# Moving the pad, two weight low parts and the turns of rows in a retention and mixture-of-experts kernel

## The chip, the cores and the metric

The kernel runs on one core of a Trainium2 chip. The metric is the device time of one execution in microseconds; the median of three runs is compared. A core has TensorE (PE; matmuls and transposes), VectorE (DVE), ScalarE (ACT), GpSimd (POOL) and SyncE (SP, which here only issues transfers). Each takes its instructions in program order, and they wait for each other on semaphores.

## The reference

Retention (linear attention with a decay for each head) over 4 batches, 8 heads, 768 positions and a head size of 64, then a layer that sends each of the 3072 tokens to one of 8 experts:

```
state = gamma * state + k_t (outer) v_t ;  y_t = scale * q_t @ state        # for each batch, head, position
x = y as 3072 rows of 512
logits = normalized(x) @ normalized(expert_emb).T / tau
e = argmax(logits) ;  gate = softmax(logits)[e]
out = gate * (relu(x @ w1[e]) @ w2[e])                                      # w1: 512 x 1024, w2: 1024 x 512
```

## The kernel before

**Retention.** The 12 blocks of 256 tokens (three for each batch) run through one loop, `for m in range(NM)`. A turn of the loop makes the masked scores of block m (`scores`, `masks`), the product with the earlier state (`inter`) and within the block (`intra`), and transposes block m+1 for the next turn (`transpose_k`, `transpose_q`). `take` copies the result to SBUF as yT (ScalarE). One turn later `rows` transposes yT into token rows on VectorE (L478) and writes them to a DRAM buffer xd by four transfers (L485), and `logits_products` and `logits_rows` make the routing scores. The tile that the row transposes write has two buffers.

**Routing.** Blocks form four groups of three. For a complete group `sums`, `choose`, `add_counts` (together `pick`), `count`, `ranks` and `split_ranks` find each token's expert and its place in the expert's list; `put_scores` writes the scores to xd; `marks_of`, `mark` and `table` turn places into a table of token numbers, with matmuls of marks. Group 2 (blocks 6 to 8) is complete in block 9 (`urgent`), and its table in block 10. The last group is done after the loop.

**The first expert starts early.** From the tokens of the first nine blocks, `early_gather` fetches 288 rows of expert 0 in block 10 (three indirect gathers issued by GpSimd, L657). `pad` (L649, L651) adds to the count of expert 0 where it has fewer than 288 such tokens: it is a matmul, one instruction for ex, and three one-column instructions of VectorE on cum. In block 11 the fetched rows are transposed and split (`rows_T`).

**Split products.** Matmuls of the expert layers work on numbers split into a high and a low part: ScalarE casts (xh at L678, whi at L229, hh at L253), and a subtraction makes the low part (xl at L679, wlo at L234, hl at L256), on VectorE unless an engine is named. Each product is three matmuls: high by high, and two with a low part. `split_cast` casts one piece of 128 x 1024 weights and returns the function for its low part; `load_piece` loads a piece into one of four raw buffers. Pieces 0 to 3 are w1 of expert 0; pieces 4 to 7 are its w2. Before the change, block 10 casts pieces 0 and 1 at its beginning and 2 and 3 at its end; in block 11 the low parts of 0, 1 and 2 go to GpSimd and that of 3 to VectorE.

**After the loop** the first layer of expert 0 (`products`, advanced by `run(n)`, n matmuls at a time) is interleaved with the last group's routing, then its second layer (`layer2`), and the experts 1 to 7, in order of their size, follow. Their rows are gathered, written to DRAM (xs) and read back in quarters (xg), transposed and split.

The order on every engine (TensorE, VectorE, ScalarE, GpSimd, SP) is that of the program text; no planner changes it. SP's queue holds all loads of weights and all writes of rows in that order.

Of the kernel before, what the change touches and what calls it, by code (L numbers as in the profile page):

```python
# [24 lines left out]
P = 128  # L25
# [7 lines left out]
NE = 8  # L33
# [78 lines left out]
def retention_moe(ctx: ExitStack, tc: tile.TileContext, q, k, v, emb, tau, w1, w2, const, const16, out):  # L112
# [56 lines left out]
    def pt_():  # L169
        npt[0] += 1  # L170
        return bank(turn_of[npt[0] % len(turn_of)])
# [340 lines left out]
    def sums(g):  # L512
        nm = len(GROUPS[g])
        ps = pt_()
        for i in range(NQ):
            nc.tensor.matmul(ps[i * Q:(i + 1) * Q, :2 * nm * NE], C("quarters"),
                             parts[g][:, :nm, :, i, :NE].rearrange("p m u e -> p (m u) e"), start=True, stop=True,
                             skip_group_check=True)
        return ps[:, :2 * nm * NE].rearrange("p (n e) -> p n e", e=NE)

    def choose(g, z):
        r = span(g)
        nb = r.stop - r.start
        bc = lambda t: t.unsqueeze(2).broadcast_to([P, nb, NE])
        m = ap_.tile([P, nb], F32, name="m", bufs=1)
        nc.vector.tensor_reduce(out=m, in_=z, axis=AX.X, op=ALU.max)
        yield
        nc.vector.tensor_tensor(out=zd[:, r], in0=z, in1=bc(m), op=ALU.subtract)
        yield
        w = ap_.tile([P, nb, NE], F32, name="w", bufs=1)  # L530
        nc.vector.scalar_tensor_tensor(out=w, in0=zd[:, r], scalar=0.0,
                                       in1=C("e16").unsqueeze(1).broadcast_to([P, nb, NE]), op0=ALU.is_lt, op1=ALU.add)
        yield
        nc.vector.tensor_reduce(out=wmn[:, r], in_=w, axis=AX.X, op=ALU.min)
        yield
        nc.vector.tensor_tensor(out=oh[:, r], in0=w, in1=bc(wmn[:, r]), op=ALU.is_equal)
        yield
# [10 lines left out]
                             skip_group_check=True)  # L548
        return pr

    def add_counts(g):
        r = span(g)
        sm = ap_.tile([P, NE], F32, name="sm", bufs=1)
        nc.vector.tensor_reduce(out=sm, in_=oh[:, r].rearrange("p c e -> p e c"), axis=AX.X, op=ALU.add)
        yield
        nc.vector.tensor_tensor(out=cum[:, r.stop], in0=cum[:, r.start], in1=sm, op=ALU.add)
        yield
# [85 lines left out]

    def pad():

        ex = cp.tile([P, 1], F32, name="ex")
        pc = pt_()
        nc.tensor.matmul(pc[:, :NE], ones, cum[:, NBE], start=True, stop=True)
        nc.vector.tensor_scalar(out=ex, in0=pc[:, :1], scalar1=-1.0, scalar2=float(EARLY), op0=ALU.mult, op1=ALU.add)  # L649
        for i in range(3):  # L650
            nc.vector.scalar_tensor_tensor(  # L651
                out=cum[:, NBE, :1], in0=ex, scalar=C("tok")[:, i:i + 1], in1=cum[:, NBE, :1],
                op0=ALU.is_gt, op1=ALU.add)
# [192 lines left out]

    def pick(g, z):
        run_all(choose(g, z))
        run_all(add_counts(g))

    for m in range(NM):
        nxt = m + 1 < NM
        done = last_of.get(m - 1)
        urgent = m == NM - 3
        py_of(m)
        if m == NM - 2:
            first = [split_cast(), split_cast()]

        if m == 0:
            psc = [scores(0, u, range(2)) for u in range(2)]  # L860
            for u in range(2):
                scores(0, u, range(2, KT), psc[u])
        for u in range(2):
            o = masks(psc[u] if m == 0 else scores(m, u), u)
            if u == 0:
                i = o[0]
        if m == 0:
            for j in (*load_q(2), load_k(2)):
                after(j, i)
            nc.sync.dma_start(out=cst2, in_=const[:, _C1:])  # L870
            nc.sync.dma_start(out=cst16, in_=const16)
        if m:
            scale_ahead(m, i)
        if urgent:
            load_piece()
            load_piece()
        if m and m + 3 < NM:
            for j in load_q(m + 3):
                after(j, i)
        if m == 0:  # L880
            state(0)
            state_copy(0)
            state_sums(0)
            next(emb_steps)
            scale_ahead(0, i)
            intra(0, 0)
            intra(0, 1)
            transpose_k(1, 0)
            i = transpose_k(1, 1)
            after(load_v(2), i)  # L890
            inter(0)
            transpose_q(1, 0)
            i = transpose_q(1, 1)
            for j in (*load_q(3), load_k(3), load_v(3)):
                after(j, i)
            state(1)
            state_copy(1)
            state_sums(1)
        else:
            inter(m)  # L900
            if nxt:
                i = state(m + 1)
                state_copy(m + 1)
                if m + 3 < NM:
                    after(load_k(m + 3), i)
            if waiting is not None and m < NM - 2:
                run_all(ranks(waiting, count(waiting)))
            if urgent or not nxt:
                x = rows_turn(m - 1 - (not nxt))
                rows(m - 1 - (not nxt), x=x)  # L910
            logits_rows(m - 1, logits_products(m - 1))
            if nxt:
                if m == NM - 2:
                    marks_of(tail - 1)
                    mark(tail - 1, range(6))
                if not urgent:
                    state_sums(m + 1)
                transpose_k(m + 1, 0)
                transpose_q(m + 1, 0)
                if urgent:  # L920
                    pick(done, sums(done))
                    state_sums(m + 1)
                    put_scores(done)
                i = transpose_q(m + 1, 1)
                if m + 3 < NM:
                    after(load_v(m + 3), i)
                if m == NM - 2:
                    table(tail - 1)
                    gathered = early_gather()
                transpose_k(m + 1, 1)  # L930
                if m == NM - 2:
                    spread_v(m + 1, 0)
                if m < NM - 3:
                    rows(m - 1)
                if m in (5, 8):
                    mark(group_of[m - 3], range(6))
                if done is not None and not urgent:
                    pick(done, sums(done))
                    put_scores(done)
                intra(m, 0)  # L940
                if urgent:
                    run_all(ranks(done, count(done)))
                    split_ranks(done)
                intra(m, 1)
                if m in (5, 8):
                    table(group_of[m - 3])
                if m in (4, 7):
                    split_ranks(waiting)
                    marks_of(waiting)
                if m == NM - 2:  # L950
                    load_piece(gathered)
                    load_piece(gathered)
            else:
                pad()
                intra(m, 0)
                for f in (*first, lows[0]):
                    f(nc.gpsimd)
                lows[1]()
                intra(m, 1)
                ps = [turn_rows(xge, EROWS, kt, bank(f"pst{kt}")) for kt in range(2)]  # L960
        waiting = done
        take(m)
        if m < NM - 2:
            spread_v(m + 1, 0)
            spread_v(m + 1, 1)
        if m == NM - 2:
            spread_v(m + 1, 1)
            lows = [split_cast(), split_cast()]
        if m == 0:
            next(emb_steps)  # L970
        if m == NM - 1:
            xh0, xl0 = (hp.tile([P, KT, CAP], F32R, name=n) for n in ("xh", "xl"))
            for kt in range(KT):
                rows_T(xge, EROWS, kt, slice(0, EARLY), ps[kt] if kt < 2 else None)
            nc.gpsimd.tensor_copy(out=zs[0][:, :3], in_=xge[:, :, DM:DM + NE])

        for _ in range(LOADS.count(m)):
            load_piece()
# [20 lines left out]
    m, g = NM - 1, len(GROUPS) - 1  # L999
    pl = logits_products(m)  # L1000
    logits_rows(m, pl)
    rows(m - 1)
    load_piece()
    load_piece()
    run(11)
    first_low = split_cast()
    z = sums(g)
    run_all(choose(g, z))
    run_all(add_counts(g))
    rows(m)  # L1010
    put_scores(g)
    run(21)
    pr = count(g)
# [3 lines left out]
    for o in held:  # L1017
        o()
    first_low()
    for _ in range(9):  # L1020
        next(sort_steps)
        run(1)
# [10 lines left out]
    load_expert(2)  # L1033
    run(12)
    split()
    for j, n in EROWS:
        square(xge, n, j, j)
    run(12)
    split()
    load_piece()  # L1040
# [431 lines left out]
```

## Time and profile before

| | |
|---|---|
| median of 3 runs | 404.69 us (404.46 to 405.96) |
| profiled execution | 404.54 us; span from first to last instruction 402.7 us |
| TensorE busy | 387.2 us, 96% |
| VectorE busy | 251.5 us, 62% |
| ScalarE busy | 227.2 us, 56% |
| GpSimd busy | 134.2 us, 33% |
| transfers | 88.00 MB, mean 219 GB/s |

The busy time of an engine is a sum over stages with different limits. A row of the timeline is one instruction or several merged (x and their number): start and length in us, engine, line, operation, output from inputs, with the idle time ahead of it in brackets and what ended it. Merged rows may overlap their neighbours a little, since the instructions of an engine are pipelined.

### The profile page before, as it was taken

The numbers are of one execution on the slowest core, as the hardware profiler recorded it, in microseconds if no ns is written. First come the engines' busy times: TensorE is split into PE (matmuls) and PEld (weight loads), VectorE is DVE, ScalarE is ACT, GpSimd is POOL, SyncE is SP. The second block draws the span as 40 slices with busy tenths as digits, with TensorE's granted clock in tenths as the row PEclk, the third lists the DMA queues.
The fourth block names the chain that finished last, engine by engine and source line by source line (L and its number), as shares of the span: only waits on it lengthen the run. The fifth ranks groups of instructions, "written<-read, shape, count | busy, mean of one in ns | idle before, by whom it ended". The sixth has DMA issues, their size and how long they took to land.

```text
span 402.7 us, 9504 instructions
## 1 busy us (share of the span) xinstructions
PE 387.2 (96%) x3652; PEld 354.8 (88%) x3652; DVE 251.5 (62%) x557; ACT 227.2 (56%) x402; POOL 134.2 (33%) x145
## 2 busy tenths in 40 slices
PE   7999999999959999999999999999999999999992
PEld 3988888888739988999999999999889889999971
DVE  4565776777798958744861864487277546576400
ACT  4687787877935256463553843664485545463410
POOL 2666544551550253311702620350273062001131
PEclk9999999999969999999999999999999999999999
DMA  7999999999358669697879677887979887933121
GB/s 214 282 298 290 256 266 248 257 248 237 75 158 215 210 192 294 199 258 207 273 220 228 223 245 209 237 311 209 256 254 334 215 245 234 244 115 100 30 101 52
DMA packets 86469, 88.00 MB, mean 219 GB/s; under 512 B 9184, under 2 KB 65120, under 8 KB 86416
## 3 DMA queue, kind: packets, MB, share of 16 engines
q1 hardware_dynamic: 81936, 74.32, 66.6%
q0 software_dynamic: 4304, 12.93, 9.4%
q8 instruction: 30, 0.49, 0.5%
q14 instruction: 23, 0.19, 0.1%
q10 hardware_dynamic: 176, 0.07, 0.1%
HBM read 65.00 MB, written 18.43 MB: 207 GB/s over the span
## 4 chain that ended last, share of the span: by engine, by line
PE 75%; DVE 11%; DMA 5%; SPq 3%; issue 2%; POOL 1%; ACT 1%; POOLq 0%; DVEq 0%
PE pst L247 10%; PE b L247 9%; PE py L247 8%; PE py L451 7%; PE b L1168 7%; PE b L387 6%; PE py L1118 5%; PE py L1168 4%; PE b L1118 4%; PE pst L1118 3%; PE b L356 3%; PE pst L421 3%; DMA xg<-xs 2%; PE b L374 2%; DVE wlo L234 2%
## 5 line engine op out<-in xcount | busy, mean ns | idle before, releaser
L234 DVE TENSOR_TENSOR wlo<-raw,whi 128x1024 fp32r<-128x1024 f32 x61 | 74.5, 1221 | 20.4 <-ACT whi L229 15.1
L1150 POOL DMA_INDIRECT out_dram<-og,si x28 | 31.0, 1108 | 126.8 <-ACT og L1143 71.7
L229 ACT CAST whi<-raw 128x1024 fp32r<-128x1024 f32 x64 | 66.2, 1044 | 1.6 <-DMA raw<-in_moe_w_dram 1.6
L407 DVE TENSOR_TENSOR pm<-b,mask 128x512 f32<-128x512 f32 x48 | 29.8, 684 | 17.0 <-PE b L387 17.0
L1099 DVE STREAM_TRANSPOSE xt<-xg 128x384 f32<-128x384 f32 (+1 forms) x28 | 15.7, 579 | 34.8 <-DMA xg<-xs 34.7
L657 POOL DMA_INDIRECT xr<-xd,gi x24 | 31.5, 1311 | 16.0 <-DMA raw<-in_moe_w_dram 8.8
L350 POOL TENSOR_TENSOR hl<-wlo,cst 128x512 f32<-128x512 f32 x22 | 22.5, 1043 | 35.3 <-DVE pm L407 24.3
L247 PE MATMUL pst<-xl,whi 128*128 128x380 f32 (+7 forms) x96 | 32.3, 336 | 0.3 <-DVE xl L1106 0.3
L247 PE MATMUL pst<-xh,wlo 128*128 128x380 f32 (+7 forms) x96 | 32.1, 334 | 0.1
L247 PE MATMUL pst<-xh,whi 128*128 128x380 f32 (+7 forms) x96 | 32.1, 334 | 0.0
L247 PE MATMUL py<-xl,whi 128*128 128x288 f32 (+7 forms) x80 | 26.9, 337 | 4.3 <-DVE xl L679 4.3
L1100 ACT CAST xh<-xt 128x408 fp32r<-128x408 f32 (+6 forms) x28 | 14.2, 510 | 23.1 <-DVE xt L1099 22.9
L247 PE MATMUL b<-xh,whi 128*128 128x408 f32 (+7 forms) x80 | 26.8, 335 | 0.0
L247 PE MATMUL py<-xh,whi 128*128 128x288 f32 (+7 forms) x80 | 26.8, 335 | 0.0
L247 PE MATMUL py<-xh,wlo 128*128 128x288 f32 (+7 forms) x80 | 26.7, 334 | 0.0
L247 PE MATMUL b<-xl,whi 128*128 128x408 f32 (+7 forms) x80 | 26.7, 333 | 0.0
L247 PE MATMUL b<-xh,wlo 128*128 128x408 f32 (+7 forms) x80 | 26.6, 333 | 0.0
L253 ACT ACTIVATE hh<-pst 128x380 fp32r<-128x380 f32 (+7 forms) x24 | 11.6, 484 | 25.1 <-PE pst L247 25.1
L387 PE MATMUL b<-qT,kT 64*128 64x128 f32 x384 | 24.9, 279 | 0.0
L273 POOL TENSOR_TENSOR r<-r,half 128x4 f32<-128x4 f32 (+1 forms) x9 | 8.9, 993 | 47.4 <-DVE r L272 47.2
L253 ACT ACTIVATE hh<-py 128x288 fp32r<-128x288 f32 (+7 forms) x20 | 9.3, 471 | 26.8 <-PE py L247 26.8
L387 PEld LDWEIGHTS b<-qT,kT 64*128 64x128 f32 x384 | 22.6, 188 | 1.7 <-issue 1.0
(246 smaller groups left out, 1053.3 us busy)
## 6 DMA issues: line engine op xcount, KB each, us to landing
raw<-in_moe_w_dram SPq DMA_DIRECT2D x60, 512.0 KB, 5.2
whi<-in_q_dram SPq DMA_DIRECT2D x24, 256.0 KB, 4.6
xd<-x SPq DMA_DIRECT2D x48, 128.0 KB, 4.6
wlo<-in_k_dram SPq DMA_DIRECT2D x11, 512.0 KB, 5.4
xs<-xr SPq DMA_DIRECT2D x6, 768.0 KB, 4.1
whi<-in_v_dram SPq DMA_DIRECT2D x6, 512.0 KB, 5.7
wlo<-in_v_dram SPq DMA_DIRECT2D x6, 512.0 KB, 5.6
xg<-xs SPq DMA_DIRECT2D x16, 192.0 KB, 4.5
```

Source lines behind the costliest of these rows:

```text
L229: nc.scalar.copy(out=hv, in_=rv)
L234: eng.tensor_tensor(out=lv, in0=rv, in1=hv.bitcast(F32), op=ALU.subtract)
L247: nc.tensor.matmul(acc[:, :w], a[:, f], x[:, kt, cols], start=(n == 0), stop=(n == 3 * KT - 1))
L253: nc.scalar.activation(out=hh[:, ft, cols], in_=acc[:, :w], func=AF.Relu)
L350: return eng.tensor_tensor(out=ks_r[:, m % 3, s, h], in0=kin[m % 3][:, h, s], in1=w[:, h], op=ALU.mult)
L387: nc.tensor.matmul(psc[a][:, j], kTs[m][a * D:(a + 1) * D, j, u].rearrange("p s c -> p (s c)"), q_cols(m, a, j, u), start=True, stop=True, ...
L407: o.append(nc.vector.tensor_tensor(out=pm, in0=psc[a], in1=w, op=ALU.mult))
L451: nc.tensor.matmul(pys[m][b][o * D:(o + 1) * D, j], lhsT, rhs, start=first, stop=True, skip_group_check=True)
L657: return nc.gpsimd.indirect_dma_start(out=xr[:n, j, :], out_offset=None, in_=xd[:rows_, :], in_offset=bass.IndirectOffsetOnAxis(ap=gi[:n, ...
L1118: nc.tensor.matmul(acc[:, :c], a[:, f], x[:, kt, :c], start=(n == 0), stop=(n == 3 * FT - 1))
L1150: i = nc.gpsimd.indirect_dma_start(out=out[:, :], out_offset=bass.IndirectOffsetOnAxis(ap=si[:n, e, j:j + 1], axis=0), in_=og[:n, j, :], i ...
L1168: nc.tensor.matmul(acc[:s, :], x[:, kt, at], a, start=(n == 0), stop=(n == 3 * FT - 1))
```

## The change

pad's place moves from block 11 to block 10, behind the early gather; its ex lies in the PSUM bank of its matmul. Of the first four low parts, two are made by VectorE in block 10 and two by VectorE in block 11. The cast of piece 1 moves behind the transposes of block 10. In `choose`, the comparison and the addition that were one instruction are two, and their results, as the sum in `add_counts`, lie in the PSUM bank of the scores. `marks_of` of group 2 moves from block 10 to the end of block 9, its marks go ahead of the logits' transposes of block 9, its table ahead of the transposes of q. Weight pieces 2 and 3 are loaded behind the rows of block 8 and the scores of group 2 in SP's queue, no longer ahead of them. The rows of blocks 9, 10 and 11 are each turned one place later, all after the loop, and the square sums of the early rows earlier.

```diff
--- before.py
+++ after.py
@@ -516,20 +516,24 @@
             nc.tensor.matmul(ps[i * Q:(i + 1) * Q, :2 * nm * NE], C("quarters"),
                              parts[g][:, :nm, :, i, :NE].rearrange("p m u e -> p (m u) e"), start=True, stop=True,
                              skip_group_check=True)
-        return ps[:, :2 * nm * NE].rearrange("p (n e) -> p n e", e=NE)
-
-    def choose(g, z):
+        return ps
+
+    def columns(ps, i, nb):
+        return ps[:, i * P:i * P + nb * NE].rearrange("p (n e) -> p n e", e=NE)
+
+    def choose(g, ps):
         r = span(g)
         nb = r.stop - r.start
         bc = lambda t: t.unsqueeze(2).broadcast_to([P, nb, NE])
+        z, below, w = (columns(ps, i, nb) for i in range(3))
         m = ap_.tile([P, nb], F32, name="m", bufs=1)
         nc.vector.tensor_reduce(out=m, in_=z, axis=AX.X, op=ALU.max)
         yield
         nc.vector.tensor_tensor(out=zd[:, r], in0=z, in1=bc(m), op=ALU.subtract)
         yield
-        w = ap_.tile([P, nb, NE], F32, name="w", bufs=1)
-        nc.vector.scalar_tensor_tensor(out=w, in0=zd[:, r], scalar=0.0,
-                                       in1=C("e16").unsqueeze(1).broadcast_to([P, nb, NE]), op0=ALU.is_lt, op1=ALU.add)
+        nc.vector.tensor_tensor(out=below, in0=z, in1=bc(m), op=ALU.is_lt)
+        yield
+        nc.vector.tensor_tensor(out=w, in0=below, in1=C("e16").unsqueeze(1).broadcast_to([P, nb, NE]), op=ALU.add)
         yield
         nc.vector.tensor_reduce(out=wmn[:, r], in_=w, axis=AX.X, op=ALU.min)
         yield
@@ -548,9 +552,9 @@
                              skip_group_check=True)
         return pr
 
-    def add_counts(g):
+    def add_counts(g, ps):
         r = span(g)
-        sm = ap_.tile([P, NE], F32, name="sm", bufs=1)
+        sm = ps[:, 3 * P:3 * P + NE]
         nc.vector.tensor_reduce(out=sm, in_=oh[:, r].rearrange("p c e -> p e c"), axis=AX.X, op=ALU.add)
         yield
         nc.vector.tensor_tensor(out=cum[:, r.stop], in0=cum[:, r.start], in1=sm, op=ALU.add)
@@ -643,8 +647,8 @@
 
     def pad():
 
-        ex = cp.tile([P, 1], F32, name="ex")
         pc = pt_()
+        ex = pc[:, P:P + 1]
         nc.tensor.matmul(pc[:, :NE], ones, cum[:, NBE], start=True, stop=True)
         nc.vector.tensor_scalar(out=ex, in0=pc[:, :1], scalar1=-1.0, scalar2=float(EARLY), op0=ALU.mult, op1=ALU.add)
         for i in range(3):
@@ -846,7 +850,7 @@
 
     def pick(g, z):
         run_all(choose(g, z))
-        run_all(add_counts(g))
+        run_all(add_counts(g, z))
 
     for m in range(NM):
         nxt = m + 1 < NM
@@ -854,7 +858,7 @@
         urgent = m == NM - 3
         py_of(m)
         if m == NM - 2:
-            first = [split_cast(), split_cast()]
+            first = [split_cast()]
 
         if m == 0:
             psc = [scores(0, u, range(2)) for u in range(2)]
@@ -871,9 +875,6 @@
             nc.sync.dma_start(out=cst16, in_=const16)
         if m:
             scale_ahead(m, i)
-        if urgent:
-            load_piece()
-            load_piece()
         if m and m + 3 < NM:
             for j in load_q(m + 3):
                 after(j, i)
@@ -905,30 +906,34 @@
                     after(load_k(m + 3), i)
             if waiting is not None and m < NM - 2:
                 run_all(ranks(waiting, count(waiting)))
-            if urgent or not nxt:
-                x = rows_turn(m - 1 - (not nxt))
-                rows(m - 1 - (not nxt), x=x)
+            if urgent:
+                rows(m - 1)
+            if m == NM - 2:
+                mark(tail - 1, range(6))
             logits_rows(m - 1, logits_products(m - 1))
             if nxt:
-                if m == NM - 2:
-                    marks_of(tail - 1)
-                    mark(tail - 1, range(6))
-                if not urgent:
+                if m < NM - 3:
                     state_sums(m + 1)
                 transpose_k(m + 1, 0)
+                if m == NM - 2:
+                    table(tail - 1)
+                    gathered = early_gather()
+                    pad()
+                    state_sums(m + 1)
+                    first[0]()
                 transpose_q(m + 1, 0)
                 if urgent:
                     pick(done, sums(done))
                     state_sums(m + 1)
                     put_scores(done)
+                    load_piece()
+                    load_piece()
                 i = transpose_q(m + 1, 1)
                 if m + 3 < NM:
                     after(load_v(m + 3), i)
-                if m == NM - 2:
-                    table(tail - 1)
-                    gathered = early_gather()
                 transpose_k(m + 1, 1)
                 if m == NM - 2:
+                    split_cast()()
                     spread_v(m + 1, 0)
                 if m < NM - 3:
                     rows(m - 1)
@@ -941,6 +946,7 @@
                 if urgent:
                     run_all(ranks(done, count(done)))
                     split_ranks(done)
+                    marks_of(done)
                 intra(m, 1)
                 if m in (5, 8):
                     table(group_of[m - 3])
@@ -951,10 +957,8 @@
                     load_piece(gathered)
                     load_piece(gathered)
             else:
-                pad()
+                lows[0]()
                 intra(m, 0)
-                for f in (*first, lows[0]):
-                    f(nc.gpsimd)
                 lows[1]()
                 intra(m, 1)
                 ps = [turn_rows(xge, EROWS, kt, bank(f"pst{kt}")) for kt in range(2)]
@@ -999,15 +1003,17 @@
     m, g = NM - 1, len(GROUPS) - 1
     pl = logits_products(m)
     logits_rows(m, pl)
-    rows(m - 1)
+    rows(m - 2)
     load_piece()
     load_piece()
     run(11)
+    for j, n in EROWS[:2]:
+        square(xge, n, j, j)
     first_low = split_cast()
     z = sums(g)
     run_all(choose(g, z))
-    run_all(add_counts(g))
-    rows(m)
+    run_all(add_counts(g, z))
+    rows(m - 1)
     put_scores(g)
     run(21)
     pr = count(g)
@@ -1017,6 +1023,8 @@
     for o in held:
         o()
     first_low()
+    rows(m)
+    square(xge, EROWS[2][1], 2, 2)
     for _ in range(9):
         next(sort_steps)
         run(1)
@@ -1033,8 +1041,6 @@
     load_expert(2)
     run(12)
     split()
-    for j, n in EROWS:
-        square(xge, n, j, j)
     run(12)
     split()
     load_piece()
```

## Rows read from the trace of the kernel before

**Rows 1.** Part 2 of the page: granted TensorE clock in 40 slices, in tenths.

```profile
PEclk9999999999969999999999999999999999999999
```

**Rows 2.** Windows: stretch, length; PE, PEld, DVE, ACT, POOL busy; clock; DMA share, GB/s.

```profile
113.80:118.07 4.27, 0.00 (x0) 0.00 (x0) 4.20 (x6) 1.04 (x1) 2.24 (x2) 0.55 0.92 261
118.07:121.09 3.02, 3.02 (x19) 2.63 (x19) 2.59 (x6) 0.00 (x0) 0.00 (x0) 0.51 0.13 30
...
160.90:200.00 39.10, 39.09 (x211) 38.86 (x212) 25.41 (x48) 20.95 (x37) 13.79 (x13) 1.00 0.78 233
```

**Rows 3.** Waits of TensorE: us in total, times, longest.

```profile
PE py L247 <- DVE xl L679: 4.3, 1, 4.3
...
PE pst L671 <- DMA xge<-xd,ri: 0.4, 1, 0.4
PE pst L1118 <- DVE hl L256: 0.4, 1, 0.4
PE pst L247 <- DVE xl L1106: 0.3, 1, 0.3
```

**Rows 4.** Timelines of VectorE and GpSimd, 108 to 119 us.

```profile
108.93 6.97 POOL L234 TENSOR_TENSOR wlo<-raw,whi 128x1024 fp32r<-128x1024 f32 x3
...
109.59 6.34 DVE L651 SCALAR_TENSOR_TENSOR cum<-ex,cst,cum 128x1 f16<-128x1 f32 x1
...
118.30 0.81 DVE L679 TENSOR_TENSOR xl<-b,xh 128x288 fp32r<-128x288 f32 x2
```

**Rows 5.** Instructions of lines L651 and L234: ns min/median/max, first and last start.

```profile
L651 DVE SCALAR_TENSOR_TENSOR cum<-ex,cst,cum x3: 222/222/6339, 109.6 to 116.2; 128x1 f16<-128x1 f32 x3
...
L234 DVE TENSOR_TENSOR wlo<-raw,whi x61: 1181/1225/1318, 116.4 to 374.6; 128x1024 fp32r<-128x1024 f32 x61
```

**Rows 6.** Timelines of VectorE and GpSimd, block 9.

```profile
87.11 2.48 DVE L407 TENSOR_TENSOR pm<-b,mask 128x512 f32<-128x512 f32 x4 [0.67 <-PE b L387]
...
87.94 2.04 POOL L350 TENSOR_TENSOR hl<-wlo,cst 128x512 f32<-128x512 f32 x2 [4.55 <-DVE pm L407]
```

**Rows 7.** Timeline of VectorE, blocks 10 and 11.

```profile
100.13 0.63 DVE L596 TENSOR_TENSOR xl<-eq,cst 128x192 f16<-128x192 f16 x2
100.67 1.06 DVE L605 TENSOR_SCALAR xh<-cst,low 128x128 f16<-128x128 f16 x6
...
105.48 2.48 DVE L407 TENSOR_TENSOR pm<-b,mask 128x512 f32<-128x512 f32 x4 [2.84 <-PE b L387]
```

**Rows 8.** Timelines of SP's queue and of GpSimd, 87 to 106 us.

```profile
87.70 9.21 SPq L202 DMA_DIRECT2D raw<-in_moe_w_dram  x16
...
99.49 1.08 SPq L624 DMA_DIRECT2D xd<-zd  x1
...
105.07 1.30 POOL L657 DMA_INDIRECT xge<-xd,ri  x1 [13.08 <-issue]
```

**Rows 9.** Timeline of ScalarE, blocks 10 and 11.

```profile
99.21 2.00 ACT L229 CAST whi<-raw 128x1024 fp32r<-128x1024 f32 x2
...
107.43 2.00 ACT L229 CAST whi<-raw 128x1024 fp32r<-128x1024 f32 x2
...
112.37 0.94 ACT L678 CAST xh<-b 128x288 fp32r<-128x288 f32 x2
```

**Rows 10.** Timeline of VectorE after the loop.

```profile
119.39 1.27 DVE L478 STREAM_TRANSPOSE x<-yT 128x512 f32<-128x512 f32 x2
121.23 0.21 DVE L526 TENSOR_REDUCE m<-b 128x6 f32<-128x48 f32 x1 [0.57 <-PE b L516]
...
136.38 0.18 DVE L618 TENSOR_TENSOR tab<-tab,b 128x32 f32<-128x32 f32 x1
```

**Rows 11.** Timelines of VectorE and GpSimd, 144 us.

```profile
144.64 1.32 DVE L234 TENSOR_TENSOR wlo<-raw,whi 128x1024 fp32r<-128x1024 f32 x1
...
144.35 0.91 POOL L657 DMA_INDIRECT xr<-xd,gi  x1 [0.30 <-issue]
```

**Rows 12.** Transfers of rows to xd (line L485): issue to landing.

```profile
DMA to landing us min/median/max: 2.0/4.6/5.8
```

## The prediction

> **What bounds the kernel now.** The page comes first. Its busy times put TensorE far ahead of all others (the table above), and its line of granted clocks is full but for one slice, the twelfth, at 0.6 [rows 1]. So the thing to find is the place where TensorE stands still. The windows by stage give it: from 113.80 to 118.07 there is no matmul at all, in the next 3.02 us the clock is at half its level (1.2 GHz), and from 160.90 on TensorE is busy 39.09 of 39.10 us [rows 2]. What is saved before 160.9 is therefore kept to the end, as long as the operands of the later stages move with it. The waits of TensorE name the cause: one wait of 4.3 us of the first expert's first layer (py L247) for a low part xl that VectorE writes at L679 [rows 3].
>
> What was VectorE doing? The timeline of VectorE and GpSimd shows it: the first of pad's three one-column instructions (L651) starts at 109.59 and lasts 6.34 us; its sisters need 0.22. Over the same time GpSimd runs its three weight low parts (L234), back to back from 108.93 to 115.90 [rows 4, 5]. The xl low parts stand behind pad in VectorE's queue and so end only at 119.1. That stretch is what the change attacks.
>
> **Why pad was held, by the rows.** L651 reads two tensors from SBUF, ex and cum, and so does GpSimd's low part. VectorE's mask products (L407) read one operand from PSUM and one from SBUF: four take 2.48 us beside GpSimd's scaling at 87.94, and four take 2.48 us at 105.48, where GpSimd only issues gathers [rows 6, 7]. So not every overlap blocks; that of two readers of SBUF did. The Trainium skill, page "SBUF — State Buffer", section "Who interferes with whom", says this as a rule: a VectorE instruction with two SBUF inputs and a GpSimd instruction that reads SBUF exclude each other, and the later one waits for the earlier to finish. By that rule pad waits for the first low part alone, 1.7 us, and its move could take no more than that out of VectorE's queue; the row shows 6.34 us, through all three, so 6.1 us, and here the measurement decides.
>
> **The change, part by part.**
> *GpSimd.* It loses its three low parts, 6.97 us [rows 4]. Nothing else that is urgent stands in its queue there.
>
> *pad in block 10.* ex now lies in PSUM, so L651 has one SBUF tensor left, and no low part runs on GpSimd. I take 0.22 us for each, 0.8 with the instruction that makes ex. The lower bound is the same; the upper bound is a wait until the early gathers end (rival 3).
>
> *Two low parts in block 10.* 1.22 us each [rows 5], with pad 3.3 us more in that block. The cover is VectorE's idle 2.84 us ahead of the masks of block 11 [rows 7], plus the time of marks_of (0.63 us of it in [rows 7]), which now fills a gap at the end of block 9. The cover of 3.5 us is just enough. Without it the masks and all behind them come up to 3.3 us later. The table is done some 1.1 us earlier, because the six marks (1.06 us [rows 7]) no longer wait for logits of block 9.
>
> *Rows of block 8 ahead of weights.* SP issued 16 weight transfers in 9.21 us from 87.70, then block 8's rows and scores; the scores' issue ended at 100.57 and the first gather started at 105.07, 4.5 later [rows 8]. With eight transfers of weights behind them instead of ahead, rows and scores go out 4.6 us earlier and land near 100.5; the table (near 101) then sets the gather, which runs from 101.2. TensorE waited only 0.4 us for it [rows 3], so no more than that is won. The weights put back are issued by about 100.5 and land 4 to 5 us later, ahead of their casts, which came at 107.4 and come no earlier.
>
> *ScalarE* now decides when the first layer starts. From its casts at 99.21 to the end of the last xh cast at 113.31 it hardly rests [rows 9], and the change leaves it the same work there: four weight casts, the copies, the xh casts. One cast moves behind the transposes, which opens small gaps; I estimate 0.3 us. The last xh is then done at 113.6, and its xl (half of the pair's 0.81 us, [rows 4]) at 114.0. VectorE has done the two remaining low parts by then (casts at 108 to 110, low parts by 111.5). Before, xl ended at 119.1: **5.0 us earlier**, rounded down.
>
> *TensorE alone* would win more: the wait of 4.3, the 0.4 for the gather, and up to half of the 3.02 us at half clock, 1.5 [rows 2, 3]: 6.2 us.
>
> *VectorE after xl* is late next. It works almost without a pause from 119.1 to 136.38, with one idle of 0.57 us [rows 10], and was already the last to arrive in the second layer, where TensorE waited 0.4 us for hl [rows 3]. Its queue changes as follows: the row transposes of block 9, which it did ahead of pad, now come behind xl, +1.27; choose has one instruction more, +0.21; the idle of 0.57 is filled [rows 10]. Those of block 11 change places, which adds nothing. That reading PSUM in choose is dearer is not to be seen: the reduction from PSUM takes 0.21 us. So tab at 136.38 moves by -5.0 + 1.27 + 0.21 - 0.57 = **-4.1 us**. TensorE, 6.2 us ahead, gives back about 2.1 us in waits for wlo and hl in the first tile of the second layer.
>
> *From there on* table, gathers of the next expert's rows and their transposes hang on VectorE and keep the 4.1; TensorE's only later wait is 0.3 us [rows 3]. The square sums move to a place where ScalarE has only one cast to do, and cost nothing; were it busy, 1.6 us.
>
> *Later rows on SP.* Rows of block 9 go out when their transposes are done, near 115.7 to 117.5, those of block 11 by 125. The gathers of the next expert, near 135, want them landed; the longest landing was 5.8 us [rows 12]. Covered by 4 us. The weights behind them go out earlier than before.
>
> Sum: 404.54 us of the profiled execution (its span and 1.84 us around it) less 4.1 is 400.4; the median of the runs lies 0.15 above that execution, so **400.6 us**.
>
> **Rivals.**
> 1. *TensorE sets the pace.* If VectorE's queue after xl shrinks more than counted (gaps inside its 17 us that the view merges), the gain runs up to TensorE's 6.2: 398.5 us. Against it: the idle shown is 0.57, and TensorE already waited for hl. Chance 0.15.
>
> 2. *The low parts in block 10 wait for the gathers.* A low part reads raw and whi, both SBUF; gathers run at 101.2 to 105.0 (the three lasted from 105.07 to the low part at 108.93, [rows 4, 8]). Held until 105.0, two low parts end near 107.4 and the masks start 2.4 us late; TensorE's intra products, the copies of yT and xh behind them follow, and xl ends about 1.1 us later: 401.7 us. For it: two SBUF readers did exclude each other [rows 4]. Against it: a low part at 144.64, beside a gather, took 1.32 instead of 1.22 us [rows 11]. Chance 0.10. The skill's page named above would allow this if an indirect gather, which reads its indices, counts as a GpSimd instruction that reads SBUF; it infers that descriptor generation is not hit, and the row at 144.64 agrees.
>
> 3. *The change does not do what it says:* pad is held by any GpSimd instruction, whatever ex lies in. It then waits for the gathers until 105.0, the low parts follow it, the masks start 3.4 us late and xl ends 2.1 us later: 402.7 us. Against it: mask products beside GpSimd are not held, nor was the low part. Chance 0.12.
>
> 4. *The clock falls again.* Fed at VectorE's pace, TensorE works in bursts between 126 and 132. Before, the two windows at about half clock lasted 7.3 us after TensorE ran dry [rows 2]; as long a stretch of work at half clock costs 3.6 us: 404.2, no change. For it: the mean of 0.55 over the first window leaves only some 0.4 us at the full level, so the clock fell soon after the last matmul. Against it: these waits are each near 1 us or less, between dense matmuls, and the waits of 0.4 us left no mark in the page's line [rows 1, 3]. Chance 0.11.
>
> 5. *Slower: the row transposes of block 11 wait for a buffer.* There are two x tiles. Block 11's takes the one that block 9's transfers read, and those now go out near 115.7 to 117.5 instead of ahead. VectorE wants it at 121.1; everything behind (marks, low parts, hl) stands in its queue. At the shortest landings (2.0 us) there is no wait, at the longest, 5.8 [rows 12], one of 2.2 us: 402.8. It cancels the gain from a landing of 7.7 us, and makes the kernel slower by over 0.5% (407 us) from near 10 us. Nothing in the rows is that long. Chance 0.04.
>
> **How the numbers follow.** Forecast 0.48, rivals 0.15, 0.10, 0.12, 0.11, 0.04. A measurement of this kernel tells about 0.5% (2 us) from no change, so faster means below 402.7. That holds the forecast, rivals 1 and 2, and half of 3, which ends on the line: 0.79; same 0.17 (rival 4 and the other half); slower 0.04. The range reaches from rival 1 to rival 3 with 0.3 us beyond the one and 0.1 beyond the other, 398.2 to 402.8, and leaves out rivals 4 and 5, 0.15.
>
> **What the profile after should show.** L651 three times near 0.22 us, near 101; 64 low parts at L234 on VectorE and none on GpSimd; early gather from about 101; no 4.3 us wait at py L247, no slice with a clock of 0.6; the last xl near 114; new waits of TensorE for wlo or hl, 2 us in all, in the first tile of the second layer; the first matmul of the second expert's first layer some 4 us earlier, and the same distance to the end from there. Wrong would be: a pad instruction of microseconds, a slice of low clock near 126 to 133, an idle VectorE ahead of the transposes of block 11, or a shift at 160 that is gone at the end.

## The result, and the profile after

The changed kernel takes 399.04 us (median of 6 runs, 397.98 to 401.56), the kernel before 405.43 us beside it (6 runs, 404.46 to 406.66): a ratio of 0.985, 95% interval 0.9815 to 0.9888, or 6.0 us less (4.5 to 7.5). The range of the forecast, 398.2 to 402.8 us, holds the time; its 4.1 us were a third too small.

The VectorE timeline of the changed kernel, where the lines of the file have moved by 4 (pad is L653 and L655, xl L683, the rows' turns still L478):

```profile
87.30 2.48 DVE L407 TENSOR_TENSOR pm<-b,mask 128x512 f32<-128x512 f32 x4 [0.68 <-PE b L387]
...
101.04 0.73 DVE L655 SCALAR_TENSOR_TENSOR cum<-b,cst,cum 128x1 f16<-128x1 f32 x3
101.69 0.41 DVE L434 TENSOR_TENSOR s<-pst,tB 128x256 f32<-128x256 f32 x1
102.02 1.22 DVE L234 TENSOR_TENSOR wlo<-raw,whi 128x1024 fp32r<-128x1024 f32 x1
103.75 1.23 DVE L234 TENSOR_TENSOR wlo<-raw,whi 128x1024 fp32r<-128x1024 f32 x1 [0.52 <-ACT whi L229]
105.09 2.49 DVE L407 TENSOR_TENSOR pm<-b,mask 128x512 f32<-128x512 f32 x4
108.44 0.45 DVE L506 STREAM_TRANSPOSE parts<-b 128x256 f32<-128x256 f32 x1 [0.86 <-PE b L498]
109.03 2.36 DVE L234 TENSOR_TENSOR wlo<-raw,whi 128x1024 fp32r<-128x1024 f32 x2
112.06 0.82 DVE L683 TENSOR_TENSOR xl<-pst,xh 128x288 fp32r<-128x288 f32 x2 [0.68 <-ACT xh L682]
112.80 0.81 DVE L683 TENSOR_TENSOR xl<-b,xh 128x288 fp32r<-128x288 f32 x2
...
113.89 1.26 DVE L478 STREAM_TRANSPOSE x<-yT 128x512 f32<-128x512 f32 x2
115.08 0.17 DVE L530 TENSOR_REDUCE m<-b 128x6 f32<-128x48 f32 x1
115.28 0.21 DVE L532 TENSOR_TENSOR zd<-b,m 128x48 f32<-128x48 f32 x1
115.41 0.20 DVE L534 TENSOR_TENSOR b<-b,m 128x48 f32<-128x48 f32 x1
...
116.75 1.30 DVE L478 STREAM_TRANSPOSE x<-yT 128x512 f32<-128x512 f32 x2
...
120.38 1.30 DVE L478 STREAM_TRANSPOSE x<-yT 128x512 f32<-128x512 f32 x2
...
131.30 0.18 DVE L622 TENSOR_TENSOR tab<-tab,b 128x32 f32<-128x32 f32 x1
```

Against [rows 4, 7, 10]: pad takes 0.73 us where its first instruction alone took 6.34; the masks of block 11 start at 105.09 (105.48), xl ends at 113.61 (119.11), tab starts at 131.30 (136.38). No turn of rows waits for a buffer.

The GpSimd and SP timelines, against [rows 8]:

```profile
101.23 1.30 POOL L661 DMA_INDIRECT xge<-xd,ri  x1 [9.06 <-DMA raw<-in_moe_w_dram]
102.83 1.27 POOL L661 DMA_INDIRECT xge<-xd,ri  x1 [0.30 <-issue]
104.41 1.37 POOL L661 DMA_INDIRECT xge<-xd,ri  x1 [0.30 <-issue]
...
92.77 1.91 SPq L485 DMA_DIRECT2D xd<-x  x4
94.78 0.43 SPq L628 DMA_DIRECT2D xd<-zd  x1
95.25 5.04 SPq L202 DMA_DIRECT2D raw<-in_moe_w_dram  x8
```

The waits of TensorE (us in total, times, longest) and the page's line of clocks, against [rows 1, 3]:

```profile
PE pst L247 <- DVE xl L1112: 0.7, 3, 0.3
...
PE pst L1124 <- DVE hl L256: 0.6, 1, 0.6
PE pst L1124 <- DVE wlo L234: 0.4, 1, 0.4
PE pst L247 <- ACT xh L1106: 0.4, 1, 0.4
...
PEclk9999999999999999999999999999999999999998
```

The wait of 4.3 us and the slice with a clock of 0.6 are gone. The waits in the first tile of the second layer (pst L1124) come to 1.0 us, 0.4 before; 2 us of new ones were expected.

**Reading runs that scatter.** The span of the profiled execution fell by only 3.9 us (402.7 to 398.8). Two places outside the change scatter: the start of block 9's masks lies between 86.5 and 89.0 us in the twelve profiles made here and the two above, with no order by kernel (of the change, only the added instruction of choose for the first two groups comes earlier); and what follows tab takes 265.8 to 267.5 us in all but one of them. The distance between the two, from the first mask of block 9 to tab (two rows of VectorE's timeline, subtracted), repeats to 0.02 us: 44.00, 44.00 and 43.98 in three profiles of the changed kernel, against 136.38 - 87.11 = 49.27 before (one profile; e1, below, which differs in one operand, has 49.22). So the change is worth **5.27 us** there, inside the interval of the times; what the medians show beyond it is not told apart from scatter.

### The profile page after: what moved, and what is told of

Read it like the earlier page. It is cut to its first block, busy times and chain, and to the rows that moved or that the text cites. A ratio compares the mean times of both kernels' runs of the same rounds, so it can differ in the third digit from the quotient of the medians.

```text
span 398.8 us, 9514 instructions
## 1 busy us (share of the span) xinstructions
PE 386.0 (97%) x3652; PEld 353.3 (89%) x3652; DVE 250.2 (63%) x564; ACT 226.9 (57%) x402; POOL 125.7 (32%) x142
## 4 chain that ended last, share of the span: by engine, by line
PE 80%; DVE 7%; DMA 6%; issue 2%; ACT 2%; POOL 1%; SPq 1%; POOLq 0%; DVEq 0%; ACTq 0%
PE pst L247 12%; PE b L247 10%; PE py L247 9%; PE py L1124 8%; PE b L1174 7%; PE py L451 7%; PE b L1124 5%; PE b L387 5%; PE pst L1124 4%; PE py L1174 4%; PE pst L421 2%; PE b L356 2%; DMA xd<-x 2%; PE b L374 2%; DMA xg<-xs 2%
## 5 line engine op out<-in xcount | busy, mean ns | idle before, releaser
L234 DVE TENSOR_TENSOR wlo<-raw,whi 128x1024 fp32r<-128x1024 f32 x64 | 78.0, 1221 | 22.8 <-ACT whi L229 17.4
L1156 POOL DMA_INDIRECT out_dram<-og,si x28 | 30.0, 1071 | 125.7 <-ACT og L1149 87.1
L661 POOL DMA_INDIRECT xr<-xd,gi x24 | 29.8, 1242 | 14.9 <-ACT sq L288 7.7
L451 PE MATMUL py<-pm,vs 128*64 128x128 f32 x384 | 23.9, 276 | 0.0
```

Source lines behind the costliest of these rows:

```text
L234: eng.tensor_tensor(out=lv, in0=rv, in1=hv.bitcast(F32), op=ALU.subtract)
L451: nc.tensor.matmul(pys[m][b][o * D:(o + 1) * D, j], lhsT, rhs, start=first, stop=True, skip_group_check=True)
L661: return nc.gpsimd.indirect_dma_start(out=xr[:n, j, :], out_offset=None, in_=xd[:rows_, :], in_offset=bass.IndirectOffsetOnAxis(ap=gi[:n, ...
L1156: i = nc.gpsimd.indirect_dma_start(out=out[:, :], out_offset=bass.IndirectOffsetOnAxis(ap=si[:n, e, j:j + 1], axis=0), in_=og[:n, j, :], i ...
```

## The experiments

All ratios are to the kernel before, run beside them. "Masks to tab" is the distance just described.

| | ratio (95% interval) | masks to tab, us | wait for an x buffer |
|---|---|---|---|
| before | 1 | 49.27 | none |
| changed | 0.985 (0.9815 to 0.9888) | 44.00 | none |
| e1 ex in PSUM alone | 0.998 (0.995 to 1.001) | 49.22 | none |
| e2 no low part on GpSimd | 0.993 (0.989 to 0.996) | 47.74 | 0.9 |
| e3 pad and low parts alone | 0.989 (0.984 to 0.994) | 45.71 | 2.9 |
| e4 gaps on GpSimd | one run, 407.82 us | 49.85 | none |
| e5 changed, again | 0.983 (0.979 to 0.987) | 44.00 | none |
| e6 changed, weights first | 0.984 (0.979 to 0.989) | 44.45 | none |
| e7 changed, turns as before | 0.979 (0.975 to 0.983) | 42.81 | none |
| e8 changed, block 9's turn as before | 0.983 (0.979 to 0.987) | 44.00 | none |
| e9 changed, both orders as before | 0.987 (0.981 to 0.992) | 46.11 | 3.3 |
| e10 e7 with ex in SBUF | 0.981 (0.976 to 0.985) | 42.81 | none |
| e11 e7 again | 0.982 (0.977 to 0.987) | 42.79 | none |
| e12 changed, third time | 0.984 (0.980 to 0.988) | 43.98 | none |

### What held pad: e1, e2, e4

e1, on the kernel before:

```diff
-        ex = cp.tile([P, 1], F32, name="ex")
         pc = pt_()
+        ex = pc[:, P:P + 1]
```

> The kernel before, with one edit: pad's ex lies in the PSUM bank of its matmul. The three low parts stay on GpSimd and pad stays in block 11. Theory (two readers of SBUF on VectorE and GpSimd exclude each other): L651 takes 0.22 us three times, but the next instruction in VectorE's queue, the low part of piece 3, reads raw and whi, both in SBUF, and takes the wait over: it starts near 110.3, lasts about 6 us and ends near 117, only 0.5 us earlier than the 117.6 before. Time 404 to 405 us, no change. Rival 1 (GpSimd's work holds any short VectorE instruction, wherever its operands lie): L651 still lasts over 6 us. Rival 2 (the exclusion ends with each GpSimd instruction): the low part of piece 3 starts near 110.3 and ends near 112.5, and the time falls by 3 us or more.

Its timelines of GpSimd and VectorE:

```profile
109.78 6.98 POOL L234 TENSOR_TENSOR wlo<-raw,whi 128x1024 fp32r<-128x1024 f32 x3
116.72 1.19 POOL L975 COPY zs<-xge 128x24 f32<-128x24 f32 x1
...
110.92 0.73 DVE L651 SCALAR_TENSOR_TENSOR cum<-b,cst,cum 128x1 f16<-128x1 f32 x3
111.64 6.21 DVE L234 TENSOR_TENSOR wlo<-raw,whi 128x1024 fp32r<-128x1024 f32 x1
```

The same three instructions, beside the same work on GpSimd, at 0.73 us for all: only where ex lies has changed. And the next reader of two SBUF tensors, the low part of piece 3, takes 6.21 us instead of 1.22 and ends at 117.85 (117.65 before). Counted from the masks of block 9 xl is 1.1 us earlier; VectorE then waits 1.2 us for TensorE ahead of ranks, and tab keeps nothing of it. Rival 1 falls, and rival 2 too.

e2, on the kernel before:

```diff
                 for f in (*first, lows[0]):
-                    f(nc.gpsimd)
+                    f()
```

> The kernel before, with one edit: the three low parts that went to GpSimd go to VectorE, at the same place in block 11; pad stays there, with ex in SBUF. Theory: with GpSimd idle L651 takes 0.22 us three times, although it still reads two tensors from SBUF; four low parts on VectorE then end near 115.1, xl near 116.7, the wait of TensorE of 4.3 us falls to about 2, tab comes 2.4 us earlier and the time is 402.3 us. Rival (the one-column instruction is slow by itself, by its type or its scalar operand): L651 lasts over 6 us here too, and with 3.7 us more work on VectorE the time is near 408.

```profile
109.12 0.74 DVE L651 SCALAR_TENSOR_TENSOR cum<-ex,cst,cum 128x1 f16<-128x1 f32 x3
109.84 4.64 DVE L234 TENSOR_TENSOR wlo<-raw,whi 128x1024 fp32r<-128x1024 f32 x4
```

With ex in SBUF and GpSimd idle, VectorE is not held. It does three low parts more and is still earlier: xl ends 2.7 us sooner counted from the masks of block 9. Of that 1.5 us is left at tab, where 2.4 was expected: VectorE waits 0.9 us for an x buffer and 0.5 for TensorE. e1 and e2 together show that it takes both, two SBUF inputs on VectorE and a low part on GpSimd.

e4 puts a memset of 128 x 32 behind each of GpSimd's low parts.

> The kernel before, with a short memset of a scratch tile on GpSimd behind each of its three low parts. It leaves nothing out. Theory A (the pair of ports is held for one instruction; it passes on as soon as GpSimd has an instruction that doesn't read SBUF): L651 begins at 109.6 and lasts until the first low part's end, near 111.3: 1.8 us. Theory B (once held, VectorE comes in only when GpSimd's queue has run dry): 6.4 us or more again, to the end of the third low part.

```profile
108.31 2.37 POOL L234 TENSOR_TENSOR wlo<-raw,whi 128x1024 fp32r<-128x1024 f32 x1
110.61 0.13 POOL L959 MEMSET gap__104<- 128x32 f32 x1
110.69 2.35 POOL L234 TENSOR_TENSOR wlo<-raw,whi 128x1024 fp32r<-128x1024 f32 x1
...
109.03 6.92 DVE L652 SCALAR_TENSOR_TENSOR cum<-ex,cst,cum 128x1 f16<-128x1 f32 x3
```

As theory B has it, VectorE doesn't get in between two low parts, with a memset of 0.13 us between them either. But the memset's record overlaps its neighbours, and the low parts stand only 0.01 us apart (110.68 to 110.69), so that a pause was hardly made; whether a longer one would let VectorE in was not tried. And "only when GpSimd's queue has run dry" is too strong. In e1 the copy at 116.72 stood behind the three low parts, and VectorE's low part, 1.22 us long when free, ended at 117.85: it began near 116.6, ahead of the copy, which lasted 1.19 us instead of 0.20. Why it got in there is not known.

(What comes after tab took 269.6 us in this one run, 2 to 4 us more than elsewhere. TensorE waited four times for xh and xl of the second expert, 1.5 us in all from 159.3, and its granted clock was 0.69, 0.50 and 0.96 in the three stretches of 2 us from 162.0, which by these numbers cost about 1.7 us. Why those rows were later is not explained.)

### What each part is worth: e3, e6 to e9

e3, on the kernel before, is the part that the prediction costed as nearly the whole gain:

```diff
                     gathered = early_gather()
+                    pad()
+                    first[0]()
                 transpose_k(m + 1, 1)
                 if m == NM - 2:
+                    first[1]()
                     spread_v(m + 1, 0)
...
-                pad()
-                intra(m, 0)
-                for f in (*first, lows[0]):
-                    f(nc.gpsimd)
+                lows[0]()
+                intra(m, 0)
                 lows[1]()
```

> The kernel before, with pad and two low parts done by VectorE in block 10 and two by VectorE in block 11, and nothing else of the change (ex in SBUF, weights ahead of rows, turns of rows, choose, marks and square sums as before). Theory (this part is the whole gain; ScalarE sets the end of xl): xl ends near 113.7, tab comes 5.4 us earlier, and the time is 399 to 400 us, that of the changed kernel or a little less. Rival (the parts around it are needed to make room in block 10): the masks of block 11 come 0.4 us or more later, the early gather lands at 111 as before and TensorE waits for it, and the gain is 3 us or less: 402 us.

xl does come 5.4 us earlier (26.56 us behind the masks of block 9, 32.00 before), as the theory has it, but tab only 3.6. The rival's sign came too, the masks of block 11 0.45 us later (18.82 us behind those of block 9, 18.37 before), and the time, 402.24 us, is the rival's 402; but it is not what held tab, since xl was on time. The VectorE and SP timelines say why:

```profile
120.73 0.71 DVE L478 STREAM_TRANSPOSE x<-yT 128x512 f32<-128x512 f32 x1 [2.87 <-DMA xd<-x]
...
111.56 0.90 SPq L208 DMA_DIRECT2D raw<-in_moe_w_dram  x2
112.56 6.14 SPq L485 DMA_DIRECT2D xd<-x  x8
```

The turn of block 11 stands 2.87 us ahead of the buffer that block 9's rows still leave from. Those rows, ready since 110.7, go out from 112.56, because SP holds them behind two weight pieces that wait for the early gather. This is the buffer wait of the prediction's rival 5, not in the changed kernel but in the one with half of the change. Neither theory had it.

The changed kernel removes that wait in two ways at once, so e6, e7 and e9 undo them one by one and together. e6 moves the two `load_piece()` of block 9 back ahead of the rows of block 8; e7 puts the turns back:

```diff
-            if urgent:
-                rows(m - 1)
+            if urgent or not nxt:
+                rows(m - 1 - (not nxt))
...
-    rows(m - 2)
+    rows(m - 1)
...
-    rows(m - 1)
+    rows(m)
...
     first_low()
-    rows(m)
```

> The changed kernel, with weight pieces 2 and 3 loaded ahead of the rows of block 8 again. Theory (the order on SP is worth no more than TensorE's wait for the early rows): the early gather starts near 105.1 as in the kernel before, lands near 111.2, TensorE waits 0.5 to 1 us for it ahead of the transposes at 110.2, and the casts of xh follow; xl ends 0.3 to 0.8 us later and the time is 0.3 to 0.8 us more than the changed kernel's. Rival (the low parts of block 10 on VectorE and the gathers get into each other's way when they meet): 1.5 us more or worse.

> The changed kernel, with the turns of rows of blocks 9, 10 and 11 at the places they had before. Theory (VectorE sets tab, and the later turns put 1.2 us into its queue where it has no rest): the turn of block 9 fits into VectorE's idle 0.86 us and 0.68 us in block 11, xl ends within 0.3 us of where it did, tab comes about 0.8 us earlier (130.5) and the time is 0.5 to 1 us less than the changed kernel's. Rival 1 (the second expert's rows set the pace by their landing, not by VectorE): tab earlier, the time the same. Rival 2 (the earlier turns cost on SP's queue or by the buffers of x): a VectorE wait ahead of a row turn, or later weights, and a longer time.

> The changed kernel with both orders as before: weight pieces 2 and 3 ahead of the rows of block 8, and the turns of rows of blocks 9 to 11 at their old places. Theory (a fast VectorE meets the x buffer: block 9's rows stand on SP behind two weight pieces that wait for the early gather, and the turn of block 11 wants their buffer): VectorE waits 1.5 to 3 us for xd<-x ahead of the turn of block 11, as in the kernel with pad and low parts alone (2.9 us), and the distance from the masks of block 9 to tab is 44.5 to 46 us, against 42.8 with only the turns put back and 44.0 in the changed kernel. Rival (the two orders act each by itself): no wait, 42.8 plus the 0.45 that the weights cost alone, 43.3 us.

Masks of block 9 to tab, us:

| | turns as before | turns later |
|---|---|---|
| weights ahead of rows of block 8 | 46.11 (e9) | 44.45 (e6) |
| rows ahead of weights | 42.81 (e7) | 44.00 (changed) |

VectorE's waits in e9 (us in total, times, longest) show the buffer again:

```profile
DVE x L478 <- DMA xd<-x: 3.3, 1, 3.3
```

The wait and the distance lie a little above the expected 1.5 to 3 us and 44.5 to 46. Either order alone takes the wait away. Rows of block 8 ahead of weights does it by an earlier gather: in e7 SP's two weight pieces go out at 106.82 and block 9's rows at 108.25, as the timelines of VectorE and SP show.

```profile
106.93 1.29 DVE L478 STREAM_TRANSPOSE x<-yT 128x512 f32<-128x512 f32 x2
...
106.82 0.90 SPq L208 DMA_DIRECT2D raw<-in_moe_w_dram  x2
108.25 8.20 SPq L485 DMA_DIRECT2D xd<-x  x8
```

The turn of block 9 fills VectorE's idle 0.86 us ahead of the logits there; the later turns, no longer needed, cost 1.19 us. e7 is the fastest version here: 397.91 us beside 399.73 (e5), and 398.86 (e11) beside 400.14 (e12) in a second comparison, with the distance 1.2 us shorter each time. Its intervals overlap those of the changed kernel; the lead rests on the two pairs of medians and the traces. The expectation of 0.5 to 1 us was a little low.

e6 alone went as its theory has it up to tab: the early gather starts 17.95 us behind the masks of block 9 (17.96 before, 13.93 in the changed kernel), xl ends 0.3 us later and tab comes 0.45 later. The longer time that was expected does not show: 399.15 us beside 399.73 (e5).

The rest of the change (ex in PSUM, choose, the places of the marks and the table, of the cast of piece 1 and of the square sums) is what e9 has more than e3: with it xl ends 0.25 us earlier and tab comes 0.40 later. No gain of it by itself is shown, and its parts were not tried one by one.

e8 puts back block 9's turn alone.

> The changed kernel, with only the turn of block 9's rows back in block 11; those of blocks 10 and 11 stay late. Theory: as with all turns at their old places, but VectorE rests near 0.9 us ahead of choose, which the turn of block 9 filled: tab only 0.3 us earlier than in the changed kernel, and the time within 0.5 us of it. Rival (the turn's transfers of block 9 go out ahead of weight pieces 6 and 7 and those come earlier or later): the casts of pieces 6 and 7 move, and TensorE's waits for wlo in the second layer with them.

44.00 again, where 0.3 us less was expected: VectorE now waits 0.98 us ahead of choose for TensorE's sums, the place that the turn had filled. The weight pieces 6 and 7 went out 5.5 us earlier (111.65 instead of 117.16), and no wait changed.

### Scatter, and ex beside the gathers: e5, e11, e12, e10

> The changed kernel again, unedited, for a second profile and more times. Theory (the step from the profiled execution's 3.9 us less of span to the 6.0 of the medians is scatter in when the second expert's rows land): the profile shows tab near 131.3 again, within 0.2 us, but the first matmul of the second expert's first layer that waits for xl at another time than 157.35, by up to 1.5 us, together with the landing of the quarters (6.17 us in the first profile). Rival (a fixed cost behind tab): 157.35 again within 0.3 us, and the same landing.

tab lay at 132.44, so the expected 131.3 was missed: the whole retention part ran 1.14 us later (masks of block 9 at 88.44, not 87.30). From there the distance is 44.00. Behind tab this run had no wait of the second expert's first layer for xl, where the first profile had 0.7 us and 0.4 for xh; the theory is right on that part.

> The changed kernel with the turns of rows at their old places, again, beside the changed kernel on the same chip. Theory: masks of block 9 to tab 42.8 us again; the times 1.2 us (0.3%) below those of the changed kernel. Rival (its lead of 1.8 us was scatter): no lead.

> The changed kernel a third time, for the comparison with the run before. Theory: masks of block 9 to tab 44.0 us again, and a time 1.4 to 1.7% below the kernel before. Rival: the distance scatters by some tenths as the times do.

Both as the theories had them: 42.79 and 43.98 us.

> The changed kernel with the turns of rows at their old places, and pad's ex back in SBUF, so that L651's counterpart reads two tensors from SBUF beside the early gathers. Theory (a gather does not hold two readers of SBUF, only GpSimd's low parts did): three times 0.22 us, masks of block 9 to tab 42.8 us, the same time. Rival (a gather holds them too): the first of the three lasts until a gather ends, 1 to 4 us, the masks of block 11 start later and the time rises by 1 to 3 us.

```profile
L655 DVE SCALAR_TENSOR_TENSOR cum<-ex,cst,cum x3: 222/223/223, 102.7 to 103.2; 128x1 f16<-128x1 f32 x3
```

The first gather starts at 102.90, between these. A gather doesn't hold a reader of two SBUF tensors; once pad is away from GpSimd's low parts, ex may lie in either memory.

## Why the prediction was right, and where it was off

*The cause.* pad was held by two SBUF inputs against GpSimd's low parts: e1 and e2 show it. The Trainium skill ("SBUF — State Buffer", "Who interferes with whom") names this exclusion, and the traces agree as to which operands it needs; that it ends with the one instruction that holds it, as the prediction read the rule, they don't bear out (6.34 us before, 6.2 and 6.4 in e1 and e4, each to the end of the third low part).

*The next bound.* VectorE's queue to tab, as forecast: TensorE waits for wlo and hl in the first tile of the second layer, and what follows tab is as long as before within the scatter: 266.3 us before, 266.0 (e5), 266.8 (e12) and 267.5 (first profile) after.

*The sum.* Forecast for tab -5.0 + 1.27 + 0.21 - 0.57 = -4.1; measured, from the masks of block 9, -5.69 + 1.19 + 0.01 - 0.74 = -5.23, within 0.04 of -5.27. Each term in turn:

- xl was mis-sized by 0.7 us: the step had the last xh cast done at 113.6, and it was done at 112.94. Each cast takes 0.40 to 0.43 us in either kernel, but before the last two fill 0.94 us [rows 9], and so do the first two, with idle between them: the transposes went only just ahead of them (those of the last two from 111.72 to 112.87), behind TensorE's wait of 0.4 us for the early rows. With the rows there in time all four fill 1.3 us instead of 2.0; in e6, where the gather is late again, the last two fill 0.94 again. The timeline of ScalarE in the changed kernel:

```profile
111.63 0.70 ACT L682 CAST xh<-pst 128x288 fp32r<-128x288 f32 x2
112.22 0.72 ACT L682 CAST xh<-b 128x288 fp32r<-128x288 f32 x2
```

- the turn of block 9: +1.19 by e7, as costed.
- the added instruction in choose: the stretch from the first of choose to the next turn takes 1.67 us (115.08 to 116.75), 1.66 before, but the instruction is not free. It (L534) starts 0.13 us behind the one ahead of it, whose result it doesn't read, where those that read the last result start 0.24 apart; in block 9 the same stretch, from m to s, grew from 1.57 us to 1.71, and in e7 this one is 1.76. In the changed kernel the turn behind it starts 0.08 us after cum, 0.18 before and in e7, which hides it. The full 0.21 us was too much; 0.10 to 0.14 is what it costs.
- idle filled: the 0.57 us, and the 0.17 ahead of ranks.

*The time.* The mechanism and the order of the bounds are as forecast, but the profiled execution's 4.0 us less (404.54 to 400.53), the forecast's own number, is luck: tab came 5.27 us earlier against the masks of block 9, and what follows tab happened to take 1.2 us longer. And 399.04 us is nearer to rival 1's 398.5 than to the forecast's 400.6; it is the waits for wlo and hl that tell the two apart.

*Rivals.* TensorE waited 1.0 us for VectorE in that tile, 0.4 before, not 2.1 more, so rival 1 was nearer than its chance said; e7, with 1.19 us less in VectorE's queue, has a wait of 0.4 there and 6.46 us less to tab, about TensorE's 6.2. Rivals 2 and 3 are refuted: the low part at 102.02 and pad at 101.04, each beside a gather, took 1.22 and 0.73 us. Rival 4 didn't come: TensorE's two waits of 0.4 and 0.6 us left the clock full. Rival 5 had the right place and the wrong kernel (e3, e9).

*The step on SP* said that rows ahead of weights win no more than 0.4 us. That about holds where the turns are late (0.45, e6); with the old turns the same order is worth 3.3 us, which the prediction did not see, since it took the buffer of x as given.

## What to carry to other kernels

Before work is shared between VectorE and GpSimd, look at where the operands lie: here two SBUF inputs on VectorE beside GpSimd's low parts stopped VectorE until the last of three was over, and moving one operand to PSUM or the work to one engine freed it. When a queue gets faster, ask which buffer it then meets; here, with pad and the low parts moved alone, the wait went to a buffer that a transfer still read, and the change holds two remedies for it where one is enough and the other has a price. Where runs scatter, measure a change as the distance between two of its own instructions.

## What the runs showed of the hardware

- A VectorE low part slows the gathers beside it, not the reverse: the second and third early gather take 1.27 and 1.37 us on GpSimd in the changed kernel, where e6 shows 1.00 and 0.93, with masks or nothing beside them; in e3 the first takes 1.86 instead of 1.30. The low parts beside gathers take 1.22 and 1.23 us in the changed kernel; the longest seen is the 1.32 of [rows 11].
- The exclusion works the other way too: in e1 GpSimd's copy of 128 x 24 lasts 1.19 us beside VectorE's low part, where 0.20 is usual.
- A wait of TensorE of 2.1 us (e2) cost as long a stretch at half clock, about 7 us, as the 4.3 us wait (the granted clock falls about 1.0 us after the last matmul in e2, 0.4 before, and is full again 5.7 and 3.0 us after the matmuls resume), so the shorter wait left more work at half clock. The changed kernel's two, of 0.4 and 0.6 us, left the clock full; in e4 it fell after four, of 0.7, 0.2, 0.3 and 0.3 us.
